# Sparse attention into a soft mixture of experts on one core: a head's strided values in one transfer, weights issued at other places, a new table of steps

## The chip, the cores and the metric

One core of one Trainium2 chip runs the whole program; the other cores are idle. The metric is the device time of one execution in microseconds (us). Three executions of the kernel before took 278.09, 280.34 and 276.68 us, a median of 278.09. The execution that was profiled took 276.79 us.

## The reference: what is computed

Everything is float32. Attention has 8 batches, 8 heads, 576 positions and a head size of 64. Heads 0 to 3 are local: a position sees itself and the 31 before it. Heads 4 to 7 are strided: a position sees itself and every 32nd position before it. The 4,608 attention rows of 512 columns then go through a soft mixture of 8 experts with 4 slots each:

```python
scores = scale * np.matmul(q, k.transpose(0, 1, 3, 2))
scores = np.where(masks[None, :, :, :], scores, -1000000000.0)   # local or strided, by head
attn = softmax(scores); x = matmul(attn, v) as [4608, 512]
logits = x @ phi                              # [4608, 32]
d = exp(logits - logits.max(0)); d /= d.sum(0) + 1e-09
slot_input = (d.T @ x).reshape(8, 4, 512)
h = np.maximum(slot_input[e] @ w1[e], 0.0)    # w1: 8 x 512 x 1024
slot_out[e] = h @ w2[e]                       # w2: 8 x 1024 x 512
c = softmax of logits over the 32 slots; out = c @ slot_out
```

The inputs q, k and v have 9.4 MB each, w1 and w2 16.8 MB each, and the output has 9.4 MB.

## The kernel before

**Quads.** Attention runs in 16 quads. Quad i is half of batch i // 2: two local heads (L) and two strided heads (S). Each quad loads four pieces of 256 KB from q and k: kL, qL, kS, qS (`emit_D`, line 262), each into one of three slots of the tile natb that are used in turn. GpSimd (POOL) copies a slot into a second place of natb (`emit_g`, line 292), which sets the slot free for the load three places later in the order kL, qL, kS, qS. TensorE (PE) transposes the copy (line 297), ScalarE (ACT) brings it out of PSUM, and PE computes the scores SL and SS (line 339). VectorE (DVE) adds the mask (line 374) and does the softmax with ACT; PE transposes the probabilities (line 409) and multiplies them by the values (line 417: AA, AS, AL). DVE scales the result (line 445). After that come transposes of the result (line 463), logits (line 493) and the running sums of the expert inputs.

**Values.** The local values of a quad go to tile vb with two transfers (`emit_Dv`, line 272), and in even quads two more for the strided heads (line 275). POOL makes a shifted copy of them (`emit_C2`, lines 287 and 288). The strided values of a quad go to the tile vs (`emit_Ds`, lines 281 and 282): for each of two heads one transfer of 32 rows and one of 4 rows of 4 KB. There is one tile vs, so the values of quad i can be loaded only when AS of quad i - 1 is through. In even quads two transfers bring the first 64 positions of k and q (`emit_Dt`, line 267).

**Weights.** The 64 pieces of w1 and w2 have 512 KB each (`load_weights`, lines 230 and 236). 28 have buffers of their own and are issued among the quads. 14 more go into buffers that attention has finished with (`alias`), three into buffers that are set up at its end, and 19 into buffers whose first piece has been used.

**Order.** All loads and stores but four at the start are issued by one in-order queue, that of SyncE (SP). A load whose slot isn't free holds everything behind it. Each load also waits until the eighth load before it has landed, since eight semaphores are used in turn. The order on every engine comes from one table, `PHASE`: step n of quad i stands at 10 i + PHASE[n], and all steps are issued sorted by that number; names with z are for the last quad. The 28 first pieces of weights are spread evenly over a stretch of this scale (line 807).

**After attention.** The merge of the running sums and the first layer (line 751) and second layer (line 848) of the experts follow, then the output (lines 880 to 901).

Of the kernel before, what the change touches and what calls it, by code (L numbers as in the profile page):

```python
# [19 lines left out]
B, H, S, D = 8, 8, 576, 64  # L20
# [6 lines left out]
NI = 36  # L27
NWBUF = 28
# [2 lines left out]

PER = 10.0
PHASE = dict(
    Tt=3.0549, et=4.3395, kcL=7.2375, kcS=8.7312, gkL=0.2559, gqL=0.8303, TkL=2.855, ekL=5.2515, gkS=2.8985,
    TqL=1.0809, eqL=1.3885, gqS=5.0649, TkS=4.7896, ekS=9.2422, TqS=6.9164, eqS=9.3388, SL=8.8442, SS=9.7154,
    a2=12.5045, aA=10.9105, a1=10.5397, m2=12.6538, m1=11.6053, b2=13.0014, b1=12.5329, EX2=17.5591, EX1=14.8092,
    PA=15.0999, fA=19.7117, PL=15.5347, fL=20.5771, s2=18.0977, s1=19.1961, rc=20.5093, PS=20.6197, fS=21.1914,
    AL=24.2833, AA=24.0248, nA=31.4594, nL=26.6825, AS=24.1782, nS=25.8726, XS=27.7017, xS=30.7485, XL=30.3671,
    xL=31.079, XB=32.3997, xB=32.6207, LG=33.7627, lc=34.5846, T9=32.8537, x9=33.5214, G9=34.1179, lg=34.7042,
    c9=34.9164, bm=35.2119, ED=35.582, E9=37.2234, EA=37.8204, DT=38.4714, dt=39.0128, zz=38.8764, z9=52.716,  # L40
    SI=39.5339, S9=40.2453, ac=46.699, Dt=0.8707, DkL=0.0, DqL=0.3016, DkS=2.3875, DqS=3.0779, C2=21.76, Dv=20.5822,
    Ds=21.084, zv=11.529, SI0=498.5116, S90=510.6551, SI1=513.46, S91=560.2397, mt=334.2577, gm=359.5975, wP=388.6333,
    wD=389.0898, wA=397.7973, zD=495.4337, zP=508.5013, rg=541.3667, ac0=562.6124, ac1=576.8116, ms=512.6231,
    sP0=576.712, sD0=583.5026, sP1=630.7093, sD1=740.025, Px=638.6707, P0=926.8769, P1=933.8801, P2=940.6386,
    P3=949.8326, P4=979.8978, P5=1149.6072, P6=1669.1748, cT0=22.4126, cA0=245.9107, cE0=520.1564, cB0=662.2642,
    cT1=46.1015, cA1=161.9628, cE1=399.4109, cB1=851.5859, cT2=429.4962, cA2=694.6513, cE2=904.3317, cB2=993.4772,
    c0=703.3551, cU0=1425.2595, cV0=1435.6409, cU1=1425.5245, cV1=1533.9363, cU2=1361.3444, cV2=1718.6483,
    Dsz=12.8299, DkLz=-7.06, gkLz=-0.9084, TkLz=6.6403, ekLz=19.4685, DqLz=-2.6752, gqLz=-0.3103, TqLz=0.5266,
    eqLz=7.994, DkSz=7.4798, gkSz=8.9023, TkSz=11.519, ekSz=13.7977, DqSz=0.2458, gqSz=6.6062, TqSz=12.7013,
    eqSz=15.037, kcLz=6.2282, kcSz=14.2315, Dvz=12.8199, C2z=34.9949, SLz=20.7723, SSz=19.5062, PAz=124.3611,  # L50
    PLz=127.8851, PSz=58.5904, ALz=170.2782, AAz=178.1129, ASz=156.901, XSz=185.8669, XLz=189.1461, XBz=303.8504,
    LGz=207.8193, T9z=197.7644, G9z=260.0382, DTz=366.6328, a1z=82.7684, aAz=52.517, a2z=21.4935, m1z=92.2205,
    m2z=24.7947, b1z=103.8945, b2z=33.809, s1z=162.6625, s2z=112.4845, rcz=162.8392, nSz=169.6686, nLz=178.586,
    nAz=185.0709, lgz=280.662, c9z=275.0918, bmz=304.5668, zzz=395.4671, z9z=464.258, dtz=369.2408, EX1z=119.6183,
    EX2z=55.1124, fAz=161.0905, fLz=146.8446, fSz=126.5403, xLz=189.7582, xSz=186.6572, xBz=392.3765, x9z=252.9407,
    EDz=329.3454, E9z=307.7543, EAz=380.3278, Dw=0.0,
)

SEQ = "eehllllllllhllllllllsrrtrrorrorrorrorrorrrrstOOOOO"
# [26 lines left out]
def tile_sparse_attention_soft_moe(  # L86
# [12 lines left out]
    nc = tc.nc  # L99
# [10 lines left out]
    def big(nm, cols, dt=F32):  # L110
        return const.tile([P, cols], dt, name=nm)
# [9 lines left out]
    d = big("d", 128)  # L121
    d9 = big("d9", 128)
    dt = big("dt", 160)
# [77 lines left out]
    def last(x):  # L201
        return key(x.strip("-"), NQ - 1 - x.count("-"))

    alias = sorted(((max(last(x) for x in names) + .01, n, t[:, 1024 * k:1024 * k + 1024]) for n, (names, t, k) in enumerate(alias)),
                   key=lambda x: x[:2])
# [50 lines left out]
    def heads(i, s):  # L256
        h = 2 * (i % 2) + (4 if s == "S" else 0)
        return slice(h, h + 2)
# [18 lines left out]
    def emit_Ds(i):  # L277

        for a in range(2):
            src = v[i // 2, heads(i, "S")][a].rearrange("(i g) d -> i (g d)", g=16)  # L280
            nc.sync.dma_start(out=vsx(i)[a:96:3, 1024 * a:1024 * a + 1024], in_=src[0:32])
            nc.sync.dma_start(out=vsx(i)[96 + a:3 * NI:3, 1024 * a:1024 * a + 1024], in_=src[32:NI])  # L282

    def emit_C2(i):

# [110 lines left out]
    def emit_PA(i):  # L396
        t = box["PA", i] = take()
        nc.tensor.transpose(out=t[0][:, 0:128], in_=pb[:, 512:640], identity=ident)

    def emit_fA(i):  # L400
        t = box.pop(("PA", i))
        ACT(out=pta, in_=t[0][:, 0:128])
        give(t)
# [35 lines left out]
    def place(i, s):  # L439
        return (4 if i % 4 == 2 else 2 * (i % 2)) + (s == "S")  # L440
# [60 lines left out]
    def rows9(i):  # L501
        return slice(32 * (i // 4), 32 * (i // 4) + 32)
# [78 lines left out]
    def emit_SI(i, hs=(0, 1)):  # L581
        if 0 in hs:
            box["SI", i] = take()
        for h in hs:
            for t in range(4):
                lo = place(i - 1 + h, "L")
                nc.tensor.matmul(out=box["SI", i][0][32 * t:32 * t + 32, 256 * h:256 * h + 256].rearrange("p (c d) -> p c d", c=2),  # L587
                                 lhsT=dt[:, 32 * t:32 * t + 32], rhs=xn[:, lo:lo + 2, t, :],
                                 start=h == 0, stop=True, skip_group_check=True)

    def emit_S9(i, hs=(0, 1)):
        cols = slice(256 * hs[0], 256 * hs[-1] + 256)
        nc.tensor.matmul(out=box["SI", i][0][rows9(i), cols], lhsT=dt[:, 128:160],
                         rhs=x9b[:, cols], start=False, stop=True, skip_group_check=True)

    def emit_ac(i, hs=(0, 1)):
        cols = slice(256 * hs[0], 256 * hs[-1] + 256)
        t = box["SI", i]
        if i == 1:
# [18 lines left out]
    for s in "LS":  # L618
# [3 lines left out]
        fns["n" + s] = lambda i, s=s: emit_n(s, i)  # L622
        fns["X" + s] = lambda i, s=s: emit_X(s, i)
    fns.update(Dt=emit_Dt, Tt=emit_Tt, et=emit_et, Dv=emit_Dv, Ds=emit_Ds, C2=emit_C2, SL=emit_SL, SS=emit_SS, rc=emit_rc, PA=emit_PA,
               fA=emit_fA, AL=emit_AL, AS=emit_AS, AA=emit_AA, nA=emit_nA, xL=emit_xL, xS=emit_xS,
               XB=emit_XB, xB=emit_xB, LG=emit_LG, lc=emit_lc, lg=emit_lg, T9=emit_T9, x9=emit_x9, G9=emit_G9, c9=emit_c9,
               bm=emit_bm, ED=emit_ED, E9=emit_E9, EA=emit_EA, zz=emit_zz, z9=emit_z9, DT=emit_DT, dt=emit_dt, SI=emit_SI,
               S9=emit_S9, ac=emit_ac)
# [169 lines left out]
    tasks = []  # L798
# [5 lines left out]
                tasks.append((key(n, i), n, i))  # L804
    tasks += [(key(n, L), n, L) for n in once]
    for w in range(NWBUF):
        tasks.append((PHASE["Dw"] + (alias[0][0] - PHASE["Dw"]) * w / NWBUF, "w", w))
    for n, (at, _, _) in enumerate(alias):
        tasks.append((at, "w", NWBUF + n))
    tasks.sort()  # L810
# [132 lines left out]
```

## Time and profile before

| what | value |
|---|---|
| median of three executions | 278.09 us |
| the profiled execution | 276.79 us |
| its span, first to last instruction | 275.0 us |
| PE, DVE, ACT, POOL busy | 81%, 63%, 55%, 37% of the span |
| moved by DMA | 72.78 MB, 265 GB/s over the span |

The span is what the trace covers; the rest of the time, 1.79 us, lies around it. The busy share of PE is that of modelled ends of pipelined matmuls. The DMA share is the mean over the core's 16 DMA engines; values over 1 occur, since packets overlap.

### The profile page before, as it was taken

The page shows a single profiled execution, that of the slowest core. Times are in us where ns is not written, and L with a number is a line of the kernel's source. Part 1 is how long each engine was busy: PE and PEld are TensorE (multiplying, and loading weights), DVE is VectorE, ACT ScalarE, POOL GpSimd, SP SyncE. Part 2 cuts the span into 40 slices and gives each one's busy share as a digit, 9 for nine tenths or more (in the row PEclk, how much of TensorE's full clock was granted, in tenths as well). Part 3 has the DMA queues.
Part 4 walks back from the last instruction along what each step waited for, and adds up shares of the span by engine and source line. Part 5 has one row for each costly group of instructions (what it writes and reads, how often), then busy time and mean ns, then how long its engine had stood idle before and what let it go on. Part 6 is the DMA issues. An engine that isn't in the chain of part 4 may idle for free.

```text
span 275.0 us, 9678 instructions
## 1 busy us (share of the span) xinstructions
PE 223.5 (81%) x3964; PEld 172.2 (63%) x3964; DVE 172.4 (63%) x369; ACT 150.2 (55%) x310; POOL 101.4 (37%) x171
## 2 busy tenths in 40 slices
PE   4875859779999869699998997988887998998400
PEld 1754759569887758598887886776664334555300
DVE  5067647739878957667895896695985701155600
ACT  2566638728886757568778696577434011044500
POOL 5544365265337635363643653366310200000000
PEclk9999979979999999889999999999999999999955
DMA  7996988786697687879769878596999999999997
GB/s 217 328 267 169 268 235 207 221 268 216 154 305 242 156 282 230 260 199 288 233 144 310 246 219 234 164 285 178 279 345 350 357 355 348 348 354 380 333 346 269
DMA packets 81195, 72.78 MB, mean 265 GB/s; under 512 B 33536, under 2 KB 75904, under 8 KB 81152
## 3 DMA queue, kind: packets, MB, share of 16 engines
q1 hardware_dynamic: 80192, 71.84, 84.9%
q8 instruction: 31, 0.51, 0.7%
q10 hardware_dynamic: 960, 0.33, 0.7%
q14 instruction: 12, 0.10, 0.1%
HBM read 62.72 MB, written 9.44 MB: 262 GB/s over the span
## 4 chain that ended last, share of the span: by engine, by line
PE 46%; DMA 25%; SPq 7%; POOL 6%; DVE 5%; ACT 2%; issue 2%; DVEq 0%; POOLq 0%; ACTq 0%
DMA natb<-in_q_dram 9%; PE bank L297 8%; DMA natb<-in_k_dram 8%; PE bank L339 7%; PE bank L417 6%; PE bank L751 5%; DMA out_dram<-wb 5%; PE bank L848 4%; PE bank L463 3%; DMA vb<-in_v_dram 3%; POOL natb L292 3%; PE bank L409 2%; PE bank L587 2%; SPq L282 2%; PE bank L493 2%
## 5 line engine op out<-in xcount | busy, mean ns | idle before, releaser
L292 POOL COPY natb<-natb 128x512 f32<-128x512 f32 x64 | 41.2, 649 | 73.5 <-DMA natb<-in_k_dram 40.4
L297 PE MATMUL bank<-cf,natb 128*128 128x128 f32 x288 | 47.3, 295 | 22.8 <-POOL natb L292 17.0
L297 PEld LDWEIGHTS bank<-cf,natb 128*128 128x128 f32 x288 | 34.8, 150 | 30.3 <-POOL natb L292 22.1
L374 DVE TENSOR_TENSOR pb<-bank,cb 128x512 f32<-128x512 f32 (+2 forms) x48 | 22.3, 469 | 20.0 <-PE bank L339 19.4
L445 DVE TENSOR_TENSOR xnb<-bank,rz 128x512 f32<-128x512 f32 x32 | 21.5, 688 | 11.0 <-PE bank L417 10.2
L316 ACT COPY qtb<-bank 128x512 f32<-128x512 f32 x32 | 18.9, 590 | 16.1 <-PE bank L297 15.6
L382 DVE TENSOR_TENSOR pb<-pb,mx 128x640 f32<-128x640 f32 (+1 forms) x32 | 27.2, 850 | 0.5
L339 PE MATMUL bank<-kLb,qtb 128*32 128x128 f32 x576 | 23.7, 293 | 0.1
L287 POOL COPY vb<-vb 64x1024 f32<-64x1024 f32 x16 | 16.6, 1040 | 19.2 <-DMA vb<-in_v_dram 18.8
L316 ACT COPY kSb<-bank 64x512 f32<-64x512 f32 x32 | 20.0, 626 | 4.9 <-PE bank L297 4.2
L389 DVE TENSOR_REDUCE rz<-pb 128x8 f32<-128x288 f32 (+1 forms) x32 | 21.0, 678 | 2.3 <-ACT pb L386 2.0
L379 DVE TENSOR_REDUCE mx<-pb 128x10 f32<-128x640 f32 (+1 forms) x32 | 22.0, 688 | 0.5
L386 ACT ACTIVATE pb<-pb 128x640 f32<-128x640 f32 (+1 forms) x32 | 19.1, 596 | 4.0 <-DVE pb L382 3.8
L467 ACT COPY xtb<-bank 128x512 f32<-128x512 f32 x16 | 9.4, 588 | 21.6 <-PE bank L463 21.5
L463 PE MATMUL bank<-cf,xnb 128*128 128x128 f32 x128 | 20.8, 289 | 0.0
L339 PEld LDWEIGHTS bank<-kLb,qtb 128*32 128x32 f32 x576 | 17.9, 117 | 4.4 <-issue 2.5
L316 ACT COPY kLb<-bank 64x512 f32<-64x512 f32 x32 | 20.3, 634 | 0.4
L413 ACT COPY ptb<-bank 128x512 f32<-128x512 f32 x32 | 19.1, 597 | 1.6 <-PE bank L409 1.3
L409 PE MATMUL bank<-cf,pb 128*128 128x128 f32 x128 | 19.3, 273 | 0.3 <-ACT pb L386 0.3
L288 POOL COPY vb<-vb 64x1024 f32<-64x1024 f32 x16 | 18.8, 1172 | 0.7
L417 PE MATMUL bank<-vb,ptb 128*32 128x128 f32 x512 | 17.9, 273 | 1.2 <-POOL vb L288 1.2
L417 PE MATMUL bank<-vs,ptb 128*32 128x128 f32 x480 | 16.8, 274 | 1.4 <-DMA vs<-in_v_dram 1.4
(159 smaller groups left out, 407.5 us busy)
## 6 DMA issues: line engine op xcount, KB each, us to landing
wb<-in_moe_w_dram SPq DMA_DIRECT2D x47, 512.0 KB
natb<-in_k_dram SPq DMA_DIRECT2D x32, 256.0 KB
natb<-in_q_dram SPq DMA_DIRECT2D x32, 256.0 KB
vb<-in_v_dram SPq DMA_DIRECT2D x32, 144.0 KB
vs<-in_v_dram SPq DMA_DIRECT2D x30, 128.0 KB
out_dram<-wb SPq DMA_DIRECT2D x12, 256.0 KB
vb<-in_moe_w_dram SPq DMA_DIRECT2D x4, 512.0 KB
natb<-in_moe_w_dram SPq DMA_DIRECT2D x3, 512.0 KB
```

Of the source, the lines that this page charges most:

```text
L292: PC(out=nat2(x).rearrange("p (n h d) -> p h n d", n=TN, h=2), in_=nat(x, i).rearrange("p (h n d) -> p h n d", n=TN, h=2))
L297: nc.tensor.transpose(out=t[0][:, 128 * n:128 * n + 128], in_=src[:, 128 * n:128 * n + 128], identity=ident)
L316: ACT(out=dst, in_=src)
L339: nc.tensor.matmul(out=t[0][32 * c:32 * c + 32, x:x + wd], lhsT=lhsT, rhs=rhs, start=True, stop=True, skip_group_check=True)
L374: nc.vector.tensor_tensor(out=dst, in0=box[t, i][0][:, lo:lo + 2 * n * kk].rearrange("p (s k a) -> p s k a", s=n, a=2), in1=mk.rearrange(" ...
L379: nc.vector.tensor_reduce(out=part(box[i][0], w), in_=psg[w].rearrange("p s k a -> p s a k"), op=ALU.max, axis=AX.X)
L382: nc.vector.tensor_tensor(out=psg[w], in0=psg[w], in1=over(box[i][0], w), op=ALU.subtract)
L389: nc.vector.tensor_reduce(out=part(box[i][1], w), in_=psg[w].rearrange("p s k a -> p s a k"), op=ALU.add, axis=AX.X)
L409: nc.tensor.transpose(out=t[0][:, 128 * r:128 * r + 128], in_=pb[:, lo + 128 * r:lo + 128 * r + 128], identity=ident)
L417: nc.tensor.matmul(out=t[0][32 * c:32 * c + 32, 128 * r:128 * r + 128], lhsT=lhsT, rhs=rhs, start=True, stop=True, skip_group_check=True)
L445: nc.vector.tensor_tensor(out=xn[:, place(i, s)].rearrange("p r (a d) -> p r a d", a=2), in0=t[0].rearrange("p (r a d) -> p r a d", r=4, a=2),
L463: nc.tensor.transpose(out=t[0][:, 128 * r:128 * r + 128], in_=xn[:, place(i, s), r, :], identity=ident)
```

## The change

`emit_Ds` loads the strided values of a head with one transfer of 36 rows where there was one of 32 and one of 4. The 28 first weight pieces start at 12 on the table's scale and are spread over 135 (two new entries, Dw and Dx), where they started at 0 and were spread up to the place of the first piece that goes into a finished buffer, 162.7. All other entries of the table have new numbers.

```diff
-    SI=39.5339, S9=40.2453, ac=46.699, Dt=0.8707, DkL=0.0, DqL=0.3016, DkS=2.3875, DqS=3.0779, C2=21.76, Dv=20.5822,
-    Ds=21.084, zv=11.529, ...
+    SI=42.072, S9=42.9712, ac=60.2767, Dt=3.0029, DkL=0.0, DqL=0.1732, DkS=2.2475, DqS=3.8327, C2=24.3868, Dv=20.0962,
+    Ds=21.8081, zv=19.7227, ...
...
-    EDz=329.3454, E9z=307.7543, EAz=380.3278, Dw=0.0,
+    EDz=479.8308, E9z=482.5148, EAz=585.4793, Dw=12.0, Dx=135.0,
...
-            src = v[i // 2, heads(i, "S")][a].rearrange("(i g) d -> i (g d)", g=16)
-            nc.sync.dma_start(out=vsx(i)[a:96:3, 1024 * a:1024 * a + 1024], in_=src[0:32])
-            nc.sync.dma_start(out=vsx(i)[96 + a:3 * NI:3, 1024 * a:1024 * a + 1024], in_=src[32:NI])
+            nc.sync.dma_start(out=vsx(i)[a:3 * NI:3, 1024 * a:1024 * a + 1024],
+                              in_=v[i // 2, heads(i, "S")][a].rearrange("(i g) d -> i (g d)", g=16))
...
-        tasks.append((PHASE["Dw"] + (alias[0][0] - PHASE["Dw"]) * w / NWBUF, "w", w))
+        tasks.append((PHASE["Dw"] + PHASE["Dx"] * w / NWBUF, "w", w))
```

In the orders below, lines of the change after 281 have a number one lower than before.

The order on SP around quad 10, before, from its load of kL on: natb rows with 128x2x256 are kL, qL, kS, qS in this order, wb rows are weights, vb rows (lines 272, 275) are the values of quad 8, vs rows its strided values.

```order
L262 DMA natb<-in_k_dram 128x2x256
L262 DMA natb<-in_q_dram 128x2x256
L272 DMA vb<-in_v_dram 64x9x64 x2
L275 DMA vb<-in_v_dram 64x2x64 x2
L267 DMA natb<-in_k_dram 64x8x64
L267 DMA natb<-in_q_dram 64x8x64
L281 DMA vs<-in_v_dram 32x1024
L282 DMA vs<-in_v_dram 4x1024
L281 DMA vs<-in_v_dram 32x1024
L282 DMA vs<-in_v_dram 4x1024
L262 DMA natb<-in_k_dram 128x2x256
L262 DMA natb<-in_q_dram 128x2x256
```

The same loads in an even quad of the change, from kL to the two weights that follow qS:

```order
L262 DMA natb<-in_k_dram 128x2x256
L272 DMA vb<-in_v_dram 64x9x64 x2
L275 DMA vb<-in_v_dram 64x2x64 x2
L262 DMA natb<-in_q_dram 128x2x256
L280 DMA vs<-in_v_dram 36x1024 x2
L262 DMA natb<-in_k_dram 128x2x256
L267 DMA natb<-in_k_dram 64x8x64
L267 DMA natb<-in_q_dram 64x8x64
L262 DMA natb<-in_q_dram 128x2x256
L230 DMA wb_104<-in_moe_w_dram 128x1024
L230 DMA wb_105<-in_moe_w_dram 128x1024
```

Before, ten loads of values and of first positions stood between qL and kS; now two stand there, and the others lie between kL and qL and between kS and qS. In some quads of the change one of the two weights stands behind qL.

The order on SP at the start of the program, before:

```order
L262 DMA natb<-in_k_dram 128x2x256
L230 DMA wb_89<-in_moe_w_dram 128x1024
L262 DMA natb<-in_q_dram 128x2x256
L267 DMA natb<-in_k_dram 64x8x64
L267 DMA natb<-in_q_dram 64x8x64
L262 DMA natb<-in_k_dram 128x2x256
```

and in the change:

```order
L262 DMA natb<-in_k_dram 128x2x256
L262 DMA natb<-in_q_dram 128x2x256
L262 DMA natb<-in_k_dram 128x2x256
L267 DMA natb<-in_k_dram 64x8x64
L267 DMA natb<-in_q_dram 64x8x64
L262 DMA natb<-in_q_dram 128x2x256
L262 DMA natb<-in_k_dram 128x2x256
L262 DMA natb<-in_q_dram 128x2x256
L230 DMA wb_89<-in_moe_w_dram 128x1024
```

The first weights moved from between kL and qL of quad 0 to behind qL of quad 1.

PE in one quad of the change (quad 3), from the transposes of kL and qL on: line 416 is AS and AL of quad 1, then come the transposes of kS (296), the probabilities PL of quad 2 (408), and the results of quad 1 (462).

```order
L296 MATMUL bank_124<-cf,natb 128x128 x4
L296 MATMUL bank_120<-cf,natb 128x128 x4
L416 MATMUL bank_119<-vs,ptb 32x128 x16
L416 MATMUL bank_123<-vb,ptb 32x128 x16
L296 MATMUL bank_121<-cf,natb 128x128 x4
L408 MATMUL bank_122<-cf,pb 128x128 x4
L462 MATMUL bank_118<-cf,xnb 128x128 x4
L462 MATMUL bank_124<-cf,xnb 128x128 x4
```

Before, the same quad stood like this from the transposes of qL on, with an older result (482), kL (297) and logits (493) between qL and the values (417):

```order
L297 MATMUL bank_117<-cf,natb 128x128 x4
L482 MATMUL bank_122<-cf,xtb 128x128 x4
L297 MATMUL bank_124<-cf,natb 128x128 x4
L493 MATMUL bank_119<-xtb,phs 32x128 x8
L417 MATMUL bank_123<-vb 32x128 x4
L417 MATMUL bank_121<-vs,ptb 32x128 x16
L417 MATMUL bank_117<-vb,ptb 32x128 x16
L297 MATMUL bank_118<-cf,natb 128x128 x4
```

AS and AL now follow directly on the transposes of kL and qL, and the older result and the logits stand at the end of a quad.

## Rows read from the trace of the kernel before

**Rows 1.** Engines by stretch: us, busy us (instructions), clock, DMA share, GB/s.
```profile
32.40:175.10 142.70, 125.41 (x2533) 109.72 (x2529) 106.66 (x225) 99.96 (x207) 70.72 (x122) 0.96 0.78 231
195.10:212.70 17.60, 14.12 (x189) 9.99 (x192) 13.26 (x38) 7.60 (x19) 2.04 (x2) 1.00 1.06 340
212.70:242.00 29.30, 28.14 (x342) 12.26 (x341) 8.77 (x23) 4.23 (x10) 1.85 (x2) 1.00 1.07 352
```

**Rows 2.** The chain that ended last, shares of the span by engine.
```profile
PE 46%; DMA 25%; SPq 7%; POOL 6%; DVE 5%; ACT 2%; issue 2%; DVEq 0%; POOLq 0%; ACTq 0%
```

**Rows 3.** Timeline of DVE, mask added to SL (line 374): start, us, operation.
```profile
32.43 1.11 DVE L374 TENSOR_TENSOR pb<-bank,cb 128x512 f32<-128x512 f32 x2 [1.36 <-PE bank L339]
...
151.92 0.63 DVE L374 TENSOR_TENSOR pb<-bank,cb 128x512 f32<-128x512 f32 x1
161.44 0.84 DVE L374 TENSOR_TENSOR pb<-bank,cb 128x512 f32<-128x512 f32 x2
175.10 0.63 DVE L374 TENSOR_TENSOR pb<-bank,cb 128x512 f32<-128x512 f32 x1
```

**Rows 4.** Waits of the SP queue: us in total, times, longest us.
```profile
SPq L262 <- POOL natb L292: 22.4, 20, 3.7
SPq L262 <- DMA natb<-in_k_dram: 17.9, 17, 2.5
```

**Rows 5.** Timeline of SP, loads of qL and kS in quads 10 to 12.
```profile
110.77 0.37 SPq L262 DMA_DIRECT2D natb<-in_q_dram  x1
...
119.80 0.39 SPq L262 DMA_DIRECT2D natb<-in_k_dram  x1
...
123.41 0.37 SPq L262 DMA_DIRECT2D natb<-in_q_dram  x1
...
129.02 0.38 SPq L262 DMA_DIRECT2D natb<-in_k_dram  x1
...
135.18 0.37 SPq L262 DMA_DIRECT2D natb<-in_q_dram  x1
```

**Rows 6.** Loads by source line: issue time in ns, min/median/max.
```profile
L262 SPq DMA_DIRECT2D natb<-in_k_dram x32: 367/383/869, 0.7 to 179.4; - x32
L230 SPq DMA_DIRECT2D wb<-in_moe_w_dram x28: 340/457/1224, 1.2 to 178.9; - x28
L272 SPq DMA_DIRECT2D vb<-in_v_dram x32: 618/677/1480, 17.1 to 187.8; - x32
L267 SPq DMA_DIRECT2D natb<-in_k_dram x8: 602/688/1777, 2.2 to 161.1; - x8
L281 SPq DMA_DIRECT2D vs<-in_v_dram x30: 522/574/1760, 22.0 to 184.1; - x30
L282 SPq DMA_DIRECT2D vs<-in_v_dram x30: 612/662/736, 22.7 to 184.6; - x30
```

**Rows 7.** Chain in order of time, loads on it: start (the issue), us until landed.
```profile
26.69 8.67 DMA natb<-in_k_dram
107.97 6.50 DMA natb<-in_q_dram
```

**Rows 8.** Timeline of SP, start of the program.
```profile
1.24 0.46 SPq L230 DMA_DIRECT2D wb<-in_moe_w_dram  x1
...
17.08 2.15 SPq L272 DMA_DIRECT2D vb<-in_v_dram  x2
...
24.71 0.39 SPq L262 DMA_DIRECT2D natb<-in_k_dram  x1
```

**Rows 9.** Timeline of SP, first weights into a finished buffer.
```profile
186.68 0.34 SPq L230 DMA_DIRECT2D natb<-in_moe_w_dram  x1
```

**Rows 10.** Timeline of PE, one quad's AS: start, us, operation.
```profile
187.99 1.08 PE L417 MATMUL bank<-vs,ptb 128*32 128x128 f32 x32
```

**Rows 11.** Waits of PE on the strided values: us in total, times, longest us.
```profile
PE bank L417 <- DMA vs<-in_v_dram: 1.4, 3, 0.7
```

More of the change, by code (lines that the diff above doesn't have):

```diff
@@ L33 @@
 PHASE = dict(
[L34 to L38, printed above, removed]
@@ L39 @@
-    xL=31.079, XB=32.3997, xB=32.6207, LG=33.7627, lc=34.5846, T9=32.8537, x9=33.5214, G9=34.1179, lg=34.7042,
-    c9=34.9164, bm=35.2119, ED=35.582, E9=37.2234, EA=37.8204, DT=38.4714, dt=39.0128, zz=38.8764, z9=52.716,
-    SI=39.5339, S9=40.2453, ac=46.699, Dt=0.8707, DkL=0.0, DqL=0.3016, DkS=2.3875, DqS=3.0779, C2=21.76, Dv=20.5822,
-    Ds=21.084, zv=11.529, SI0=498.5116, S90=510.6551, SI1=513.46, S91=560.2397, mt=334.2577, gm=359.5975, wP=388.6333,
-    wD=389.0898, wA=397.7973, zD=495.4337, zP=508.5013, rg=541.3667, ac0=562.6124, ac1=576.8116, ms=512.6231,
@@ L44 @@
[L44 to L53, printed above, removed]
@@ L54 @@
-    nAz=185.0709, lgz=280.662, c9z=275.0918, bmz=304.5668, zzz=395.4671, z9z=464.258, dtz=369.2408, EX1z=119.6183,
-    EX2z=55.1124, fAz=161.0905, fLz=146.8446, fSz=126.5403, xLz=189.7582, xSz=186.6572, xBz=392.3765, x9z=252.9407,
-    EDz=329.3454, E9z=307.7543, EAz=380.3278, Dw=0.0,
+    Tt=9.6038, et=10.3851, kcL=10.6681, kcS=13.4452, gkL=0.9329, gqL=4.1757, TkL=6.3774, ekL=6.871, gkS=6.8735,
+    TqL=6.5093, eqL=7.6895, gqS=7.7116, TkS=9.5313, ekS=10.8295, TqS=11.5569, eqS=12.6624, SL=13.1617, SS=13.8697,
@@ new lines @@
+    a2=16.1595, aA=15.6276, a1=15.2446, m2=22.5778, m1=15.6544, b2=22.7903, b1=15.7826, EX2=22.8531, EX1=17.2133,
+    PA=20.768, fA=26.2608, PL=19.5322, fL=24.1996, s2=25.5401, s1=24.4269, rc=26.1887, PS=25.0952, fS=25.7614,
+    AL=27.7842, AA=32.4081, nA=34.668, nL=29.4779, AS=26.9326, nS=29.2546, XS=29.8997, xS=32.0539, XL=30.3309,
+    xL=32.7287, XB=36.347, xB=39.5187, LG=34.6051, lc=35.0032, T9=35.5834, x9=35.9459, G9=36.5682, lg=37.5003,
+    c9=37.7397, bm=37.7859, ED=38.684, E9=37.8455, EA=39.1839, DT=40.241, dt=41.5441, zz=42.4115, z9=42.7798,
@@ new lines @@
+    SI=42.072, S9=42.9712, ac=60.2767, Dt=3.0029, DkL=0.0, DqL=0.1732, DkS=2.2475, DqS=3.8327, C2=24.3868, Dv=20.0962,
+    Ds=21.8081, zv=19.7227, SI0=679.5928, S90=762.3624, SI1=715.0478, S91=797.762, mt=467.9924, gm=537.767,
+    wP=657.1821, wD=704.0405, wA=708.9741, zD=765.8409, zP=834.8393, rg=907.504, ac0=847.2662, ac1=1123.2861,
+    ms=833.2169, sP0=938.8331, sD0=943.5361, sP1=1209.9617, sD1=1367.5121, Px=1011.1248, P0=1167.6355, P1=1305.9386,
+    P2=1427.4815, P3=1625.2873, P4=1626.8701, P5=1727.8045, P6=1751.0926, cT0=19.1153, cA0=24.4842, cE0=139.0474,
@@ new lines @@
+    cB0=1371.0201, cT1=35.2472, cA1=183.0501, cE1=295.6139, cB1=367.5496, cT2=504.0438, cA2=737.564, cE2=901.4265,
+    cB2=1186.4764, c0=814.1453, cU0=1639.1368, cV0=1830.225, cU1=516.042, cV1=1153.8345, cU2=1355.4236, cV2=1807.0237,
+    Dsz=19.7327, DkLz=-1.9121, gkLz=2.9256, TkLz=5.3473, ekLz=24.0234, DqLz=6.6829, gqLz=11.2532, TqLz=11.4762,
+    eqLz=20.0676, DkSz=6.1417, gkSz=12.7044, TkSz=16.6045, ekSz=17.7577, DqSz=4.9644, gqSz=19.7127, TqSz=20.5368,
+    eqSz=21.7526, kcLz=16.5817, kcSz=5.1785, Dvz=13.2226, C2z=21.4225, SLz=110.613, SSz=24.3153, PAz=234.8419,
@@ new lines @@
+    PLz=197.9076, PSz=152.2631, ALz=250.78, AAz=269.2802, ASz=195.7204, XSz=286.7744, XLz=355.1806, XBz=415.2348,
+    LGz=398.2105, T9z=370.3761, G9z=408.6123, DTz=612.8808, a1z=124.2368, aAz=51.0167, a2z=64.0697, m1z=134.8659,
+    m2z=94.5922, b1z=149.8694, b2z=115.8754, s1z=198.2369, s2z=157.6556, rcz=204.5293, nSz=250.7478, nLz=260.4784,
+    nAz=361.3559, lgz=447.4962, c9z=422.8023, bmz=447.9691, zzz=668.4817, z9z=765.3048, dtz=666.0561, EX1z=176.3103,
+    EX2z=126.6132, fAz=263.318, fLz=247.5649, fSz=155.4772, xLz=374.5048, xSz=357.4052, xBz=469.7094, x9z=401.5681,
```

## The prediction

> **What bounds the kernel now.** The first view is the table of engines by stretch. After the quads, from 195 us on, the DMA share is 1.06 and 1.07 and some 350 GB/s flow [rows 1]: there the end is set by bytes, and by the moment from which they flow freely. In the stretch of the quads the share is 0.78, and no engine is full either: PE is busy 125.41 of 142.70 us. That stretch is cut by the mask additions of quad 2 and quad 14, at 32.43 and 175.10 us [rows 3], so it holds twelve quads of 11.89 us, in each of which PE is busy 10.45 us, DVE 8.89, ACT 8.33 and POOL 5.89. DMA needs 0.78 x 11.89 = 9.3 us of a quad at share 1, or 8.7 us at the 1.07 that it reaches when nothing holds it. So 1.44 us of each quad are PE's waiting.
>
> The second view is the queue of SP, which waits for slots: 22.4 us for POOL's copies and 17.9 us for earlier loads [rows 4]. Its timeline shows a loop [rows 5]. The load of qL uses the slot of the kS of the quad before. From kS to the next qL go 3.61 us (119.80 to 123.41) and 6.16 us (129.02 to 135.18): kS must land and be copied. From qL to kS go 9.03 us in an even quad (110.77 to 119.80) and 5.61 us in an odd one (123.41 to 129.02): in that time SP issues values and first positions, one after the other. The four add up to 24.41 us for two quads, 12.2 each, which is about the length of a quad. The medians of issue [rows 6] explain most of the string: in an even quad 4 x 0.677 (vb; line 275 is taken like line 272) + 2 x 0.688 + 2 x (0.574 + 0.662) + 0.38 for qL itself = 6.9 us, in an odd quad 2 x 0.677 + 2.47 + 0.38 = 4.2 us. Quads with the short string can be fast: 9.52 us from 151.92 to 161.44 [rows 3]. So two things that could lie beside each other, landing and issuing, follow each other.
>
> **The quads in the change.** Between qL and kS stand now one weight at most (0.46) and two strided transfers. A transfer of 36 rows isn't in the trace. It costs no less to issue than 32 rows (0.574) and no more than both old ones (1.236); I take 0.66, the price of the 4-row transfer, which is nearest in that it also isn't a round number of rows. So the string is 0.38 + 0.46 + 2 x 0.66 = 2.2 us, at the ends of the price 2.0 and 3.3. The rest of the string moved to between kS and the next qL, beside the landing: even quads 3 x 0.383 + 2 x 0.688 + 2 x 0.457 + 4 x 0.677 = 6.2 us, odd ones 1.15 + 0.91 + 1.35 = 3.4 us, against 3.61 to 6.16 us of landing. The longer of the two counts: about 6.2 and 4.9. The loop then needs 8.4 and 7.1 us, 7.7 on average, and some 0.7 more for gaps of 0.06 us between a dozen issues. That is under PE's 10.45 us, so PE becomes the bound. What is late next is a matter of fractions: DVE's 8.89 us and ACT's 8.33 lie in chains with PE in each quad, so I don't expect PE without any gap and take **10.6 us a quad**. The ends are 9.5, the fastest quad seen, and 11.3, in a rival below. Gain: 12 x (11.89 - 10.6) = **15.5 us**; from 7 to 28 at the ends.
>
> PE's busy time is that of modelled ends and rose where the granted clock was low (0.96 on average in this stretch, a mixture of 2.4 and 1.2 GHz), so it is more likely too high than too low as a floor. The Trainium skill ("Perfetto Trace Analysis", section "Identifying the Most-Contended Engine") goes further: busy time of matmuls is no good measure of how near PE is to its limit, since they are pipelined; busy time of weight loads is better. By that rule PE would need 109.72 / 12 = 9.1 us, the quads could fall to that, and the gain would be 33 us. The fastest quad [rows 3] speaks for something between; the sum stays at 10.6, since DVE and ACT stand in the same loop.
>
> On PE itself nothing is added. AS and AL moved to right behind the transposes of kL and qL, and results and logits to the end of the quad. That costs nothing as long as the strided values have landed by then. They are issued behind qL and one weight, a quad ahead of the AS that reads them; PE waited 1.4 us in all for such values before [rows 11]. Without that cover it is the third rival below.
>
> **The start.** Before, a weight of 0.52 MB stands ahead of qL of quad 0 [rows 8]; at 352 GB/s it takes 1.5 us. And kS of quad 2 is issued at 24.71, 7.6 us after the string at 17.08 began [rows 8]; with 2.2 us of string it goes out up to 5.4 us sooner. PE also needs the values of quad 0 before that kS, and these move by less. I take 3 us of a possible 0 to 6.9.
>
> **The end.** The first weight into a finished buffer is issued at 186.68 [rows 9], 11.6 us after the mask addition of quad 14 [rows 3], and from there the program takes 88.3 us. 36 weight pieces and the output, 28.3 MB, need 80 us at 352 GB/s. In the change the first such weight waits for AS of quad 14, which by PE's order comes about as late. I take no change, with 4 us less to 4 us more as ends: a gain cannot exceed the 8 us that aren't transfer, and the strided values of the last quad now stand behind two weights that wait.
>
> **Sum.** 276.79 - 15.5 - 3 = 258.3 us for an execution like the profiled one. The median of the runs shown is 1.3 us above that one, so I forecast **260 us**.
>
> **Rivals.**
>
> *The landing stays the bound (0.18).* The 28 weights stand closer: one per 4.8 of the table's units rather than per 5.8, so 2.07 in a quad of 10 units rather than 1.72, which is 0.5 us more of transfer per quad. A load behind two weights and a string took 8.67 us to land, one behind two weights 6.50 [rows 7]. If kS takes the former each time, the loop is 2.2 + 8.67 = 10.9 us and with gaps 11.3. Gain 12 x 0.6 + 3 = 10 us: **268** on the scale of the median. Against it: 8.7 us of a quad for DMA, plus 0.5, is still under 10.6.
>
> *The 36 rows use fewer DMA engines (0.04).* If a transfer is cut evenly among engines, 36 rows of 4 KB can lie on twelve of them, three each, where 32 lay on sixteen and four on four. A row takes one engine 4 KB / (352 / 16 GB/s) = 0.19 us. Two transfers a quad then cost up to 0.37 us on engines that had two rows; under PE's bound that is hidden (9.2 + 0.4 = 9.6 us), with the landing as bound it is 12 x 0.37 = 4.5 us: **272**. The Trainium skill ("DMA: Bandwidth & Descriptors", section "Why a DMA increments its semaphore by 16 and not by 1") states such a rule: a transfer runs on the largest number of engines up to 16 that divides its outer size, so 12 for 36 rows. No row here shows engines one by one.
>
> *The string doesn't matter (0.10).* On the chain of waits SP's issuing has only 7% and DMA 25% [rows 2]. If what stands there as landing is the pace of PE and of POOL's copies behind it, spreading the string gives only the start back: **275**, from 272 to 279. Against it: the sum of the loop of SP equals the quad.
>
> *Slower (0.08).* AS stands early in PE's order, and all of the quad stands behind it, the kS transposes above all. There is one tile for strided values, so AS (1.08 us [rows 10]), two issues (1.3 us) and a landing follow each other from quad to quad. With 8.67 us of landing [rows 7] this is 11.1 us, and it decides from a landing of 9.5 us on; with 11 us, behind a queue filled with qL and closer weights, a quad has 13.4 us, and the time is 278 + 12 x 1.5 - 3 = **293**. For it: the transfers now stand behind a weight. Against it: no landing on the chain was that long, and the waits for such values were at most 0.7 us [rows 11].
>
> **How the numbers follow.** My forecast has 0.60. The others have 0.18, 0.04, 0.10 and 0.08. A measurement of this kernel can tell about 2% from no change, that is 5.6 us: faster means under 272.5. The forecast with its ends (12 quads at 9.8 to 11.0, start and end) spans 250 to 266; the first two rivals reach to 272. So 250 to 272 holds about eight in ten. Faster: 0.60 + 0.18 and most of 0.04, 0.81. Within 2%: 0.11. Slower: 0.08.
>
> **What would show it.** In the new trace: twelve quads from the mask addition of quad 2 to that of quad 14 in some 127 us; from qL to kS on SP about 2 to 3 us; 0.6 to 0.7 us for an issue of 36 rows; PE busy for 97% of that stretch or more; the first weight into a finished buffer about 12 us behind quad 14's addition, and from there the DMA share over 1 to the end. I'd be wrong if PE waits for strided values for more than 1 us a quad, if loads land in over 7 us, or if PE is busy for less than 93% of the stretch though SP waits for slots no more.

## The result and the profile after

The changed kernel takes **257.09 us** (median; 256.50 to 262.64) against 279.21 for the kernel before: a ratio of **0.923**, with a 95% interval from 0.913 to 0.933. I had forecast 260 us, from 250 to 272. In both kernels one execution of four took 2 to 3% longer (in the change at a granted clock of 0.955 where the others had 0.974); ratios leave such executions out, medians don't, and a star in the table below marks a kernel whose profile comes from one.

The profiled execution took 256.50 us with a span of 254.7, which is 20.3 us less than before. The table of engines by stretch, cut as [rows 1] at the mask additions of quads 2 and 14 and at the first weight into a finished buffer (columns: stretch, us, busy us of PE, PEld, DVE, ACT and POOL with instructions, granted clock, DMA share, GB/s):

```profile
28.70:157.40 128.70, 122.36 (x2551) 107.35 (x2550) 108.55 (x226) 101.85 (x210) 73.33 (x125) 1.00 0.95 271
157.40:167.70 10.30, 10.04 (x220) 8.65 (x215) 9.74 (x21) 6.03 (x13) 6.34 (x11) 1.00 0.54 137
167.70:194.20 26.50, 20.94 (x341) 14.73 (x330) 21.76 (x57) 13.56 (x32) 3.97 (x4) 1.00 0.99 320
194.20:222.20 28.00, 26.80 (x327) 11.79 (x326) 4.73 (x13) 3.39 (x8) 1.84 (x2) 1.00 1.05 338
```

In the first row PE is busy 95% of the time (88% before) and the DMA share is 0.95 (0.78 before). The cuts are these additions on DVE's timeline, which answer to [rows 3], and this weight on SP's, which answers to [rows 9]:

```profile
28.71 0.69 DVE L373 TENSOR_TENSOR pb<-bank,cb 128x512 f32<-128x512 f32 x1 [0.32 <-issue]
...
157.44 0.69 DVE L373 TENSOR_TENSOR pb<-bank,cb 128x512 f32<-128x512 f32 x1 [0.23 <-PE bank L338]
```
```profile
167.67 0.34 SPq L230 DMA_DIRECT2D vs<-in_moe_w_dram  x1
```

So the gain of 20.3 us splits up: the start is 3.7 us shorter (28.71 for 32.43), twelve quads 13.9 (128.73 for 142.67, a quad 10.73 for 11.89), the way to the first such weight 1.3 (10.2 for 11.6), and the rest 1.3 (87.0 for 88.3). Of the 13.9 us, 10.9 are waiting of PE that fell away (6.3 us for 17.3) and 3.0 are less busy time of PE.

Quads 10 to 12 on SP's timeline, natb rows being kL, qL, kS, qS in turn from 95.95 on; compare [rows 5]:

```profile
95.95 0.38 SPq L262 DMA_DIRECT2D natb<-in_k_dram  x1
...
99.15 0.54 SPq L262 DMA_DIRECT2D natb<-in_q_dram  x1
99.79 1.60 SPq L280 DMA_DIRECT2D vs<-in_v_dram  x2
101.49 1.17 SPq L262 DMA_DIRECT2D natb<-in_k_dram  x1
...
108.50 0.82 SPq L262 DMA_DIRECT2D natb<-in_q_dram  x1
109.42 1.90 SPq L280 DMA_DIRECT2D vs<-in_v_dram  x2
111.42 0.45 SPq L262 DMA_DIRECT2D natb<-in_k_dram  x1
...
120.67 0.41 SPq L262 DMA_DIRECT2D natb<-in_q_dram  x1
```

From qL to kS go 2.3 and 2.9 us, where it was 9.0 and 5.6; from kS to the next qL 7.0 and 9.3, where it was 3.6 and 6.2. The string got short and the other part longer; together they are the whole way from one load of qL to the next, whatever sets its length. SP's waits at these loads are fewer: for landings 20.3 us before and 7.9 now, for POOL 23.8 and 21.8, so what fell is the waiting for landings (queue of SP, as [rows 4]; line 335 is POOL's copy of the first positions):

```profile
SPq L262 <- POOL kSb L335: 11.1, 11, 2.9
SPq L262 <- POOL natb L291: 7.8, 14, 0.7
...
SPq L262 <- DMA natb<-in_k_dram: 3.8, 3, 1.7
```

The issue of 36 rows, and PE's wait for strided values, as in [rows 6] and [rows 11]:

```profile
L280 SPq DMA_DIRECT2D vs<-in_v_dram x30: 755/789/1492, 17.4 to 161.9; - x30
```
```profile
PE bank L416 <- DMA vs<-in_v_dram: 1.9, 3, 1.2
```

### The profile page after: what moved, and what is told of

Same layout as the page of the kernel before. It is cut to its first block, busy times and chain, and to the rows that moved or that the text cites. A ratio compares the mean times of both kernels' runs of the same rounds, so it can differ in the third digit from the quotient of the medians.

```text
span 254.7 us, 9648 instructions
## 1 busy us (share of the span) xinstructions
PE 218.9 (86%) x3964; PEld 169.8 (67%) x3964; DVE 173.2 (68%) x369; ACT 151.1 (59%) x310; POOL 101.6 (40%) x171
## 4 chain that ended last, share of the span: by engine, by line
PE 46%; DMA 22%; DVE 9%; POOL 6%; SPq 5%; issue 3%; ACT 2%; DVEq 0%; POOLq 0%; ACTq 0%
DMA natb<-in_k_dram 8%; PE bank L416 8%; DMA natb<-in_q_dram 7%; PE bank L296 6%; PE bank L847 6%; PE bank L750 6%; PE bank L338 5%; DMA vs<-in_v_dram 4%; POOL natb L291 3%; PE bank L408 3%; DMA wb<-in_moe_w_dram 3%; PE bank L462 3%; PE bank L879 3%; PE bank L492 2%; SPq L267 1%
## 5 line engine op out<-in xcount | busy, mean ns | idle before, releaser
L291 POOL COPY natb<-natb 128x512 f32<-128x512 f32 x64 | 39.2, 617 | 57.9 <-DMA natb<-in_q_dram 25.9
L296 PE MATMUL bank<-cf,natb 128*128 128x128 f32 x288 | 44.1, 287 | 1.4 <-POOL natb L291 1.3
L296 PEld LDWEIGHTS bank<-cf,natb 128*128 128x128 f32 x288 | 33.7, 146 | 6.7 <-POOL natb L291 4.5
L373 DVE TENSOR_TENSOR pb<-bank,cb 128x512 f32<-128x512 f32 (+2 forms) x48 | 22.6, 473 | 13.6 <-PE bank L338 11.8
L381 DVE TENSOR_TENSOR pb<-pb,mx 128x640 f32<-128x640 f32 (+1 forms) x32 | 25.8, 805 | 1.1
L412 ACT COPY ptb<-bank 128x512 f32<-128x512 f32 x32 | 18.8, 588 | 11.6 <-PE bank L408 11.6
L408 PE MATMUL bank<-cf,pb 128*128 128x128 f32 x128 | 20.3, 281 | 2.6 <-ACT pb L385 2.5
L378 DVE TENSOR_REDUCE mx<-pb 128x10 f32<-128x640 f32 (+1 forms) x32 | 21.8, 682 | 0.6
L388 DVE TENSOR_REDUCE rz<-pb 128x10 f32<-128x640 f32 (+1 forms) x32 | 21.9, 685 | 0.3 <-ACT pb L385 0.3
L315 ACT COPY kSb<-bank 64x512 f32<-64x512 f32 x32 | 20.3, 633 | 2.6 <-ACT xnb L485 1.2
L287 POOL COPY vb<-vb 64x1024 f32<-64x1024 f32 x16 | 21.5, 1342 | 0.7
L408 PEld LDWEIGHTS bank<-cf,pb 128*128 128x128 f32 x128 | 14.1, 141 | 6.5 <-ACT pb L385 3.6
L338 PE MATMUL bank<-kSb,qtb 128*32 128x72 f32 (+1 forms) x576 | 15.5, 236 | 3.1 <-POOL kSb L335 3.0
L462 PE MATMUL bank<-cf,xnb 128*128 128x128 f32 x128 | 17.9, 275 | 0.0
```

The source lines that it names most:

```text
L287: PC(out=v2[0:64, :, 1:9], in_=v1[64:128, :, 0:8])
L291: PC(out=nat2(x).rearrange("p (n h d) -> p h n d", n=TN, h=2), in_=nat(x, i).rearrange("p (h n d) -> p h n d", n=TN, h=2))
L296: nc.tensor.transpose(out=t[0][:, 128 * n:128 * n + 128], in_=src[:, 128 * n:128 * n + 128], identity=ident)
L315: ACT(out=dst, in_=src)
L338: nc.tensor.matmul(out=t[0][32 * c:32 * c + 32, x:x + wd], lhsT=lhsT, rhs=rhs, start=True, stop=True, skip_group_check=True)
L373: nc.vector.tensor_tensor(out=dst, in0=box[t, i][0][:, lo:lo + 2 * n * kk].rearrange("p (s k a) -> p s k a", s=n, a=2), in1=mk.rearrange(" ...
```

## The experiments

Twelve more runs were made, one of them (a_again) of the change itself. "Quad" is the length of one of the twelve quads in the profile, from DVE's timeline; the two next columns are means over the quads 2 to 12 on SP's timeline; the last two are sums of waits in us over the whole profile: SP's strided loads waiting for the values matmuls of the quad before (AS), and POOL's copies waiting for PE's transposes. The kernel before has one median for each of the three sets of runs: b_merge, b_move, b_merge_move and a_split in the first, a_again, a_back, a_pe and a_dx160 in the second, the b_mm kernels and a_dx160_ds in the third; the change has the runs of its own comparison.

| kernel | median us | ratio to before (95%) | quad us | qL to kS | kS to qL | SP for AS | POOL for PE |
|---|---|---|---|---|---|---|---|
| before | 279.5, 279.5, 276.6 | 1 | 11.89 | 7.2 | 4.8 | 0.5 | 9.3 |
| b_merge* | 275.7 | 0.997 (0.990 to 1.003) | 11.70 | 6.2 | 5.6 | 0 | 4.4 |
| b_move | 270.3 | 0.983 (0.971 to 0.995) | 11.19 | 4.5 | 6.2 | 11.1 | 23.9 |
| b_merge_move* | 267.6 | 0.970 (0.957 to 0.984) | 11.34 | 3.7 | 7.2 | 17.3 | 39.6 |
| b_mm_tk* | 267.0 | 0.960 (0.947 to 0.972) | 11.29 | 4.0 | 6.8 | 21.0 | 30.5 |
| b_mm_w | 266.8 | 0.967 (0.956 to 0.978) | 11.03 | 3.3 | 7.6 | 10.3 | 26.0 |
| b_mm_tk_w* | 267.7 | 0.962 (0.947 to 0.977) | 11.24 | 3.9 | 7.2 | 17.0 | 32.0 |
| change | 257.1 | 0.923 (0.913 to 0.933) | 10.73 | 3.1 | 7.3 | 3.8 | 4.2 |
| a_again (the change) | 260.6 | 0.935 (0.928 to 0.942) | 10.51 | 2.9 | 7.3 | 3.3 | 7.8 |
| a_split | 262.8 | 0.956 (0.939 to 0.973) | 11.01 | 4.1 | 6.5 | 1.8 | 6.0 |
| a_back | 272.8 | 0.988 (0.983 to 0.994) | 11.40 | 6.1 | 5.4 | 2.5 | 5.6 |
| a_pe | 260.7 | 0.943 (0.933 to 0.953) | 10.68 | 3.1 | 7.1 | 9.7 | 9.3 |
| a_dx160 | 255.2 | 0.927 (0.919 to 0.935) | 10.33 | 2.9 | 7.2 | 3.2 | 6.0 |
| a_dx160_ds | 258.3 | 0.936 (0.928 to 0.944) | 10.43 | 1.4 | 8.6 | 1.8 | 9.4 |

**The merge alone.** The kernel before with the diff's lines of `emit_Ds` and nothing else.

> The kernel before with one transfer of 36 rows per head and nothing else. Loop theory (in the kernel before, landing of kS and the string of issues between qL and kS follow each other): the string gets shorter by 2 x (1.236 - 0.789) = 0.9 us and two gaps, 1.0 us a quad, so some 12 us over the quads: about 266, from 264 to 270. Rival (the issues are hidden behind landing or PE anyway): 276 to 280, no change. Rival (fewer DMA engines for 36 rows hurt): above 280.

Measured: no change that can be told, 0.997 (0.990 to 1.003). The string did get 1.0 us shorter, but the way from kS to the next qL got 0.8 us longer. Three of its loads on SP show it (qL, kS and the next qL of one odd quad):

```profile
99.84 0.37 SPq L262 DMA_DIRECT2D natb<-in_q_dram  x1
104.00 0.45 SPq L262 DMA_DIRECT2D natb<-in_k_dram  x1
...
108.27 0.37 SPq L262 DMA_DIRECT2D natb<-in_q_dram  x1
```

The string takes 4.2 us, less than either of [rows 5], and yet quads average 11.70 us: what a shorter string gives is waited for again elsewhere.

**The move alone, and both.** Two numbers of the table:

```diff
-Dt=0.8707 ... Dv=20.5822
+Dt=2.5 ... Dv=20.15
```

> The kernel before with two numbers of the table changed: local values between kL and qL (Dv 20.15 for 20.58), first positions between kS and qS (Dt 2.5 for 0.87). All transfers and all other engines' orders stay. Loop theory: the string between qL and kS loses 4.5 us in even and 1.5 us in odd quads, which leaves PE as the bound: quads of 10.7 us, 12 x 1.2 = 14 us less, about 264, from 260 to 268. Rival (the gain of the change comes from the order on PE and DVE or from the weights): 274 to 280.

> The kernel before with both: 36 rows in one transfer, local values and first positions moved. Loop theory: PE is the bound already after the move, so the merge adds little to it: 260 to 266, within 3 us of the move alone. Additive rival (each issue saved counts): 24 us less than before, about 254.

Measured: ratios of 0.983 for the move and 0.970 for both, a third and three fifths of the 5% that I expected of the string. With both, the string is nearly as short as in the change (3.7 us), but two waits have come up, which the kernel before had less of. First SP's own, then POOL's, in the kernel before and in b_merge_move:

```profile
SPq L281 <- PE bank L417: 0.5, 1, 0.5
...
SPq L280 <- PE bank L416: 17.3, 10, 4.3
```
```profile
POOL natb L292 <- PE bank L297: 9.3, 8, 2.5
...
POOL natb L291 <- PE bank L296: 39.6, 21, 3.9
```

SP now comes to the strided loads before AS of the quad before is through, and kS stands behind them in the queue. And POOL finds loads landed, but the place to copy them to still waits for PE's transposes. b_move and b_mm_w, which have no star, show the same two waits (11.1 and 10.3 us, 23.9 and 26.0 us).

**The change with its merge undone.** The old lines of `emit_Ds` in the changed kernel.

> The changed kernel with the strided values in 32 and 4 rows again. Loop theory: 0.9 us more of issues between qL and kS, in a loop that has some 2 us to spare a quad, so 257 to 260. Rival (the merge is what made it faster): 10 us or more slower, 267 and up. Rival (36 rows on fewer DMA engines cost something, since the DMA share in the quads is now 0.95): 252 to 256.

Measured: 262.8, a ratio of 0.956 (0.939 to 0.973), quads 11.01. By the medians that is 2 to 6 us more than the two sets of runs of the change, by the ratios 2.2 to 3.4 points, 6 to 9 us: more than the 0 to 3 us that I allowed, less than the rival's 10. The interval is apart from that of the change's own comparison and overlaps that of a_again a little. The string grew by 1.0 to 1.2 us, and quads by 0.3 to 0.5. So the merge helps in the new order, and a net loss by 36 rows is ruled out; what fewer DMA engines cost by themselves, no run shows.

**The change with the string put back.** Two numbers again, run beside the change:

```diff
-Dt=3.0029 ... Dv=20.0962
+Dt=0.18 ... Dv=20.18
```

> The changed kernel with the string put back: two numbers of its table make local values (Dv) and first positions (Dt) stand between qL and kS again, all else stays. By the loop theory as I first had it, quads grow to 11.5 and more: 267 to 271. By the move alone in the kernel before, which gave about 6 us: 262 to 265. Rival (order on PE and DVE is what counts, SP has time to spare): 256 to 259.

> The changed kernel once more, as the measure for the three kernels beside it: 255 to 259 by what was measured so far.

Measured: 272.8 beside 260.6, 0.988 beside 0.935, non-overlapping intervals. Two numbers take back 12 us by the medians, and 5.3 points, about four fifths of the gain, by the ratios. The time lies above all three ranges, while the quads, 11.40 us, are nearly those of the loop theory. The profile is 13.3 us longer than that of a_again: 10.7 more in the quads, 5.8 at the start and 3.2 less behind them. Its string, in quads 10 and 11:

```profile
108.70 0.38 SPq L262 DMA_DIRECT2D natb<-in_q_dram  x1
109.17 0.67 SPq L267 DMA_DIRECT2D natb<-in_k_dram  x1
109.89 1.21 SPq L267 DMA_DIRECT2D natb<-in_q_dram  x1
111.16 1.30 SPq L272 DMA_DIRECT2D vb<-in_v_dram  x2
112.50 1.28 SPq L275 DMA_DIRECT2D vb<-in_v_dram  x2
113.89 1.60 SPq L280 DMA_DIRECT2D vs<-in_v_dram  x2
115.59 0.93 SPq L262 DMA_DIRECT2D natb<-in_k_dram  x1
...
119.85 0.37 SPq L262 DMA_DIRECT2D natb<-in_q_dram  x1
...
123.68 0.44 SPq L262 DMA_DIRECT2D natb<-in_k_dram  x1
```

It takes 6.9 and 3.8 us. The strided values stand at its end, so AS comes to wait for them, 11.8 us in all where the change has 1.9. The whole program, and then the stretch of the quads (35.4 to 172.1 us):

```profile
PE bank L416 <- DMA vs<-in_v_dram: 11.8, 5, 4.7
...
PE bank L416 <- DMA vs<-in_v_dram: 7.1, 4, 2.6
```

In the quads PE waits 12.7 us in all (engines by stretch, as in [rows 1]):

```profile
35.40:172.10 136.70, 124.05 (x2551) 109.52 (x2546) 106.96 (x226) 101.84 (x210) 72.63 (x122) 0.98 0.85 252
```

That is against 6.3 in the change and 4.3 in a_again, so most of the waiting that came back is for late strided values. SP's waits for landings are back as well (22.3 us at line 262). The string thus costs time in two ways, by strided values that come late for an early AS and by loads that are issued late, and this run doesn't part them: a kernel with local values and first positions put back but the strided loads ahead of them was not run.

The start is also hit: the mask addition of quad 2 comes at 35.38 us, 6 to 7 us behind the change, and one wait of 4.7 us for strided values stands there.

**Weights farther apart.** One number, beside the change:

```diff
-Dw=12.0, Dx=135.0
+Dw=12.0, Dx=160.0
```

> The changed kernel with its 28 first weights spread over 160 instead of 135 of the table's units: 1.75 instead of 2.07 a quad, half a us less of transfer in each. If DMA bounds the quads now (share 0.95, loads landing in 6.6 to 8 us): quads 0.3 to 0.5 us shorter, 251 to 254. If PE bounds them: no change in the quads, 256 to 258, and not slower at the end, since the quads' last 20 us have a DMA share of only 0.5. Rival (weights must be in early to keep the end fed): 259 to 262.

Measured: 255.2 beside 260.6, quads 10.33 beside 10.51 (by ratio 0.927, 0.919 to 0.935, beside 0.935, 0.928 to 0.942: the intervals touch). Quads are 0.2 us shorter than beside it and 0.4 than in the first profile of the change; these two profiles of one kernel differ by 0.2 themselves, so the gain is not told from noise. Its quads, and those of the change in the same set of runs:

```profile
29.70:153.70 124.00, 121.20 (x2553) 107.03 (x2550) 106.45 (x227) 101.20 (x208) 73.32 (x123) 1.00 0.93 270
```
```profile
29.60:155.70 126.10, 121.83 (x2551) 107.06 (x2546) 104.89 (x227) 101.73 (x210) 72.19 (x122) 1.00 0.94 276
```

PE is busy 97.7% of the time, 10.1 us a quad. What changed is the chain that ended last. Its shares by engine over the span, in the change, in a_again and in a_dx160:

```profile
PE 46%; DMA 22%; DVE 9%; POOL 6%; SPq 5%; issue 3%; ACT 2%; DVEq 0%; POOLq 0%; ACTq 0%
PE 56%; DMA 19%; DVE 9%; POOL 3%; issue 2%; ACT 2%; SPq 1%; DVEq 0%; POOLq 0%; ACTq 0%
PE 68%; DMA 9%; DVE 6%; POOL 4%; issue 2%; ACT 2%; SPq 1%; DVEq 0%; POOLq 0%; ACTq 0%
```

Within the twelve quads, landings take 44.6 of 128.7 us of this chain in the change, 24.3 of 126.1 in a_again, and in a_dx160 none is among its 195 longest pieces (before, it was 37.6 of 142.7). So in the change PE and the landing of loads take turns on the chain, and only with the weights farther apart do the landings leave it. That PE is then the floor is read from this; no run took work off PE. This kernel has the lowest median of the study, though its lead over the change is within the noise of these runs.

**PE's old order around the values.** In the changed kernel XB=36.52, LG=36.515, lc=36.6 and AA=26.925, so that these stand between the transposes of qL and AS.

> The changed kernel with PE's order around the values as it was before: AA, the logits LG and the transposes XB between the transposes of qL and AS, AL; all else stays. Theory of the PE order: AS comes 1.3 us later, so the one tile of strided values is free later, SP waits for it with kS behind, and kS's own transposes stand later on PE: 260 to 266. Rival (only the order on SP and the merge count): 256 to 259.

Measured: 260.7 and 0.943 (0.933 to 0.953), no difference that can be told from the change beside it. The mechanism is there (SP waits 9.7 us for AS, 3.3 in a_again), but quads of 10.68 us lie between the change's 10.51 and 10.73.

**What the rest of the table gives.** Between both edits in the old order (267.6) and the change (257 to 261) lie 7 to 10 us by the medians, 3.5 to 4.7 points by the ratios. Two candidates, alone and together, in the kernel before with merge and move: kL transposed first (TkL=1.05 for 2.855), and the diff's line on weights with Dw=12 and Dx=135.

> The kernel before with the merge and the move, and one number more: kL is transposed before qL and XB (TkL 1.05 for 2.855), as in the changed kernel. In the merge and move alone, POOL waited 39.6 us for PE's transposes: kS can be copied only when the transposes of kL have emptied its place, and these stood behind those of qL and XB. If that is what is left of the gain in the quads, the wait falls to under 15 us and quads from 11.3 to 10.7: 259 to 262. If not (DVE's and ACT's order, or DMA): 265 to 269.

> The kernel before with the merge and the move, and the weights placed as in the change (start at 12, spread over 135). The start gets 1.5 to 3 us shorter; in the quads the closer weights cost up to 0.5 us each where loads are waited for. Start alone: 264 to 266. If weights are what is left of the gain: 258 to 262. If they cost more than they give: above 268.

> All three: merge and move, kL transposed first, weights as in the change. If these four edits are the whole of the change that counts, this is within 2 us of the changed kernel: 256 to 261. If the new order of DVE, ACT and POOL has a share of its own: 262 to 266.

Measured: 267.0, 266.8 and 267.7 (0.960, 0.967 and 0.962), none of them told from 267.6 (0.970): the intervals overlap. With kL first, POOL's wait for transposes fell only from 39.6 to 30.5 us. With the new places of the weights the start got no shorter: quad 2's addition came at 32.9 us, against 31.2 with merge and move. So neither brings the rest.

**Strided values behind kS.** a_dx160 with Ds=22.26 for 21.8081.

> The changed kernel with weights spread over 160, and the strided values behind kS instead of ahead of it (Ds 22.26 for 21.81). The string between qL and kS falls to one weight at most. If that string still bounds: quads from 10.3 to about 9.8, 249 to 252. If PE and DMA bound: 253 to 257, no change. If the values then come too late for AS, PE waits for them: 258 and up.

Measured: 258.3, quads 10.43 for 10.33, 0.936 (0.928 to 0.944). The string fell to 1.4 us, and kS to qL grew from 7.2 to 8.6: the string no longer bounds, which fits PE as the bound. The median lies in the third range, and that mechanism is there in part: two landings of strided values, 5.8 and 6.0 us, stand on the chain in the quads. The intervals of the two kernels overlap.

## Why the prediction was right, point by point

**What bounds the kernel before: half right.** That the place of the string counts is shown by a_back: put it back, and quads and start get longer, by 10.7 and 5.8 us. It doesn't show the loop that I described, since most of what PE waits for in those quads is strided values and not the copy of kS. And I took the sum of the two parts of [rows 5] as proof that they alone make up a quad. It proves nothing: the two are the whole way from one load of qL to the next, and they add up to about a quad in every row of the table, in a_dx160 (2.9 and 7.2) as in the kernel before. b_merge and b_move refute that this loop alone bounds. In the old order the string could be cut by 1.0 us for nothing and by 2.7 us for 0.7 us a quad, because the loads that went out sooner then waited for AS and for PE's transposes.

**The quads: the number right, 10.6 forecast, 10.73 and 10.51 measured; the mechanism in part.** The gain was 13.9 us (16.6 for a_again against the same profile of before) where I had 15.5. My 10.6 were 10.45 us of busy PE and 0.15 of waiting; measured were 10.20 and 0.53 (10.15 and 0.36 in a_again). Two misses of opposite sign nearly cancelled, and that is luck. PE became the next bound only in part: it is 95 to 97% busy, where my sign was 97% or more, and landings still stand on the chain; only with thinner weights do they leave it. The 10.45 us of [rows 1] was not a floor either: a_dx160 has quads of 10.33 us, and PE's busy time lies between 10.0 and 10.4 us a quad in the six profiles of the changed kernel and its variants with the clock at 1.00 in this stretch. The Trainium skill ("Perfetto Trace Analysis", section "Identifying the Most-Contended Engine") calls the busy time of weight loads a better measure of how near PE is to its limit than that of matmuls. The 9.1 us that I worked out by it were not reached by any kernel on the average of its quads, and how much less than 10.33 PE could do with, no run shows.

**The price of 36 rows: 0.79 us, not 0.66.** It lies between my ends, and the string came to 2.9 to 3.1 us on average rather than 2.2, with waits in it.

**The start: 3.7 us where I had 3, and not by the sum that I gave.** The string counts there, but in the old order moving it gave 1.2 us (quad 2's addition at 31.28 and 31.25 in b_move and b_merge_move), and what a_back gives back contains a wait of 4.7 us for strided values. The first weight in front of qL, my other reason, shows nothing in b_mm_w. Where the other 2.5 us come from stays open.

**The end: 2.6 us where I had none**, inside the 4 that I allowed. No experiment was made for it alone.

**The rivals.** Landings of 7.6 and 8.0 us did come, so my own sign for being wrong (over 7 us) appeared, and the first rival is right for a part of the quads: these landings stand on the chain and so were not covered. They were not there in each quad, as that rival had it, and quads stayed under its 11.3 us. All seven in the twelve quads of the change (start, us until landed):

```profile
47.01 6.62 DMA vs<-in_v_dram
...
62.86 6.80 DMA natb<-in_k_dram
...
71.38 7.67 DMA wb<-in_moe_w_dram
...
84.61 7.56 DMA natb<-in_k_dram
...
99.15 5.22 DMA natb<-in_q_dram
...
108.50 8.04 DMA natb<-in_q_dram
...
117.32 2.71 DMA natb<-in_k_dram
```

The rival of fewer engines falls as a net loss with a_split, since undoing the merge costs time. That the string doesn't matter is refuted by a_back. The slower rival, AS behind late strided values, needed the old string to cost much: it is in a_back with 11.8 us, and in the change with 1.9. Its cover is thinner than I said, though. The strided loads go out not a quad ahead of the AS that reads them but 5 to 10 us, and the first landing above is such a load:

```profile
53.77 1.08 PE L416 MATMUL bank<-vs,ptb 128*32 128x128 f32 x32 [0.58 <-DMA vs<-in_v_dram]
```

**What stays open.** 7 to 10 us of the gain by the medians belong to the rest of the table, and no experiment tells to which part. Shown is which waits stand there without it (SP for AS, 10 to 21 us; POOL for PE's transposes, 24 to 40 us), and that neither kL's transposes first, nor the weights, nor both bring it; the place of AS on PE, undone in the change, shows no cost that can be told from noise. The orders of DVE, ACT and POOL and the rest of PE's were not tried apart. Open is also how much of what a_back loses is the late strided values and how much the loop.

## What to carry to other kernels

In a queue that issues in order, ask for each group of small transfers which large load stands behind it and what that load's consumer does meanwhile; moving two table entries was worth 12 us of 273 without a byte less. But doing and undoing such a move needn't weigh the same: in the old order it gave 1.7 points of the ratio alone and 2.7 beside the merge, where undoing it in the new one cost 5.3. In the old order loads that went out sooner waited at the next shared buffers; in the new one the late strided values met an AS that had been moved forward. So judge a move both ways, and look each time at what the engines wait for, since the tuned version can have come to depend on it by another route. And before a loop of two intervals is called the bound, check that the two are not simply the whole period, as they were here.

## What the runs showed of the hardware

- Issue time on SP doesn't follow the size of a transfer: 32 rows of 4 KB take 0.574 us, 4 rows 0.662 [rows 6], 36 rows 0.789. The Trainium skill ("DMA: Bandwidth & Descriptors", section "Why a DMA increments its semaphore by 16 and not by 1") says that a transfer on fewer than 16 engines has the issuing sequencer write the rest of the count. That of these three the two whose rows don't divide by 16 are the dearer ones agrees with it; that 36 rows are dearer than 4, and that the 64 rows of lines 272 and 267 take 0.677 and 0.688 us [rows 6], doesn't follow from it. The cause isn't shown.
- A wait of PE was followed by a lower clock. In the kernel before, PE waited 2.98 us for a copy of POOL up to 37.19 us; its granted clock fell before the wait ended and was then 0.50 (1.2 GHz), and four transposes of the results took 0.85 us where they took 0.44 at 63.52 us, at a clock of 1.00 (2.4 GHz). The transposes behind the wait on PE's timeline, the engines by stretch (as in [rows 1]) at either clock, and the two groups on the chain:

```profile
37.19 1.12 PE L297 MATMUL bank<-cf,natb 128*128 128x128 f32 x4 [2.98 <-POOL natb L292]
```
```profile
38.31:39.16 0.85, 0.85 (x5) 0.85 (x5) 0.00 (x0) 0.59 (x1) 0.81 (x2) 0.50 1.04 329
63.40:64.00 0.60, 0.60 (x8) 0.60 (x6) 0.57 (x2) 0.60 (x2) 0.00 (x0) 1.00 0.90 345
```
```profile
38.31 0.85 PE bank L482 x4
...
63.52 0.44 PE bank L482 x4
```

- PE's busy time per quad fell from 10.45 to 10.20 us as the granted clock in the stretch went from 0.96 to 1.00. That the clock alone does it isn't shown: a_pe, at 1.00 too, has 10.43, and these are modelled ends.
